# The first FFN product of the front tokens: seven-product units replaced by plain blocks

## The chip, the cores and the metric

One core of a Trainium2 chip runs the whole program. The metric is device time in microseconds (us), the median of the runs shown. The engines are TensorE (PE; its weight loads are listed as PEld), VectorE (DVE), ScalarE (ACT), GpSimd (POOL) and SyncE (SP, which here only issues DMAs).

## The reference

x has 2048 tokens of width 640; all inputs are bf16. There are 32 heads of width 20, and the FFN is 1728 wide.

```
xn = layernorm(x)                                  # no weights
q, k, v = split(xn @ wqkv)                         # 32 heads
phi(t) = where(t > 0, t + 1, exp(t)) + 1e-6
kv = phi(k)^T v ;  z = sum over tokens of phi(k)   # per head
o = (phi(q) kv) / (phi(q) z + 1e-6)
s = o @ wo
g = silu(relu(xn @ w1) @ w2)
out = x + s * g
```

## The kernel before, in words

Tokens are cut into 16 tiles of 128 (t) and 4 chunks of 512 (j). The 1728 FFN features are 13 full blocks of 128 (f = 0 to 12, `NF` = 13) and 64 odd ones. The width 640 is 5 blocks of 128 (k), so a plain product of one feature block with one chunk is 5 matmuls of 128x128 by 128x512 into one of 8 PSUM banks.

A small scheduler (`Sched`) takes operations in the order in which the Python code gives them, queues each on its engine, and derives the waits from named resources (`R` is what an operation reads, `W` what it writes; `hz` gives the last readers and writers of a buffer that is used again). Each engine and each DMA queue works strictly in this written order; nothing is planned beyond it. PE is in order too.

Work that matters here:

- `LN_stats(t)`: two statistics (L469) and their combination (L473) on VectorE, then two small POOL steps (L475, L477) that make `rsy`, the reciprocal standard deviation. `LN_norm(t)` (L497) writes the normed tile `xn` on VectorE, and a DMA transpose on SP (`xnT_dma`, L546) turns it into `xnT`, features by tokens.
- Tiles 0 to 3 (chunk 0) take a quicker way at the start: they are centred only, transposed on TensorE and copied to `xcT`. What is made from `xcT` lacks the factor `rsy`, so it is scaled later. `scale_rows` and `scale_bcast` spread `rsy` of these 512 tokens over all partitions (`rsyB`), and `scale_h(f)` multiplies a feature block of the hidden layer by it on VectorE.
- A key tile: `K_mm(t)` (L556, 10 matmuls of 320 columns into two banks), `K_exp` and `K_relu` on ScalarE (L569), `K_fin` on VectorE (L585, L587).
- A query block: `Q_mm` (L609, 5 matmuls), exp and relu on ScalarE (L617, L622), two sums on VectorE.
- A plain FFN block: `H_mm` or `H_block` (L658, 5 matmuls), and relu from PSUM into `hT` on ScalarE (L662). `H_half` (L676) makes the 64 odd features of two chunks in 20 narrow matmuls.
- A seven-product unit: `h_unit(i, jp)` makes the feature blocks i and i + 6 for the two chunks 2jp and 2jp + 1 by a two-by-two scheme of Strassen's kind (Winograd's form). In place of the 20 matmuls of four plain blocks it has 18 (L1036; seven products of two, and the fifth k-block by itself in four matmuls), sums of weights (`h_S`) and of activations (`h_T`) on VectorE ahead, and copies and sums through PSUM behind (ScalarE L1042 and L1048; VectorE L827).

Before the change the order is: chunk 0 as far as the keys of tiles 0 to 3, from `xcT`; five plain FFN blocks of chunk 0 (f = 4, 5, 10, 11, 12, the list `HP`) from `xcT`; key tiles 4 to 7; the same five blocks of chunk 1; `H_half(0)`; two query blocks; four units `h_unit(0..3, 0)` for the front pair of chunks, with key tiles 8 to 11 and query blocks between their steps; key tiles 12 to 15 with query blocks; two query blocks of chunk 2. Then the second pair of chunks follows with six units `h_unit(0..5)`, and all the rest (the key-value products, the second FFN product and the output product, most of it on L882 in seven products too). A key tile that stands inside a unit carries one more matmul (L562, `whole`), which fills the rest of its bank.

The x loads go to 8 slots (`xin`); `xs(t)` tells which. The units need a buffer for their fifth product, `s5h`.

Of the kernel before, what the change touches and what calls it, by code (L numbers as in the profile page):

```python
# [208 lines left out]
def bass_recurrent_scan__linear_attn_block__dense_activation_relu__prompt_kernel(  # L209
# [107 lines left out]
    rsyH = nc.alloc_sbuf_tensor("rsyH", [P, 4], f16)  # L317
    rsyB = wv_flat[:, 2 * D:2 * D + 4 * P].bitcast(f16)
    s5h = [wv_flat[:, 0:1024].bitcast(f32), wv_flat[:, 2 * D + 4 * P:2 * D + 4 * P + 1024].bitcast(f32)]
# [49 lines left out]
    def xs(t):  # L369
        return t if t < XR else (t - 4) % XR  # L370

    def x_load(t, n=1, E="SP", extra=()):
        sl = xs(t)
        dma(E, lambda eng: eng.dma_start(xin[:, sl:sl + n, :],
                                         x2[P * t:P * (t + n), :].rearrange("(t p) n -> p t n", p=P)),
            W=[("xin", sl + i) for i in range(n)], extra=extra)
# [36 lines left out]
    w1_load(2, 3, "SP")  # L413
    w1_load(5, 6, "SP")
    x_load(4)
    x_load(5)
    w1_load(6, NW, "SP")
    x_load(6)
    x_load(7)
    for d in (0, 3):  # L420
        w1_load(d, d + 1, "SP")
# [29 lines left out]
    def build_mv6():  # L451
        for lo, n, off in ((0, 6, 0), (6, 2, P - 2 * DH)):
            mt = mv6[:, lo:lo + n]
            key = ("mv6", lo)
            sc.op("POOL", lambda eng, mt=mt: eng.memset(mt, SC), W=[key])
            sc.op("POOL", lambda eng, mt=mt, n=n, off=off: eng.affine_select(
                out=mt, in_=mt, compare_op=ALU.is_ge, fill=0.0, base=-off, pattern=[[-DH, n]], channel_multiplier=1),
                R=[key], W=[key])
            sc.op("POOL", lambda eng, mt=mt, n=n, off=off: eng.affine_select(
                out=mt, in_=mt, compare_op=ALU.is_ge, fill=0.0, base=off + DH - 1, pattern=[[DH, n]], channel_multiplier=-1),  # L460
                R=[key], W=[key])

    build_consts()

    def bn(t, a):
        xv = xin[:, xs(t), :]
        sc.op("DVE", lambda eng: eng.bn_stats(stats[:, t, a, :], xv[:, HN * a:HN * (a + 1)]),  # L469
              R=[("xin", xs(t))], W=[("stats", t, a)])  # L470
# [16 lines left out]
    def LN_norm(t):  # L487
        if t >= 99:
# [4 lines left out]
                out=xn[:, t, :], in_=xin[:, xs(t), :], func=ACTF.Identity, bias=rsv[:, t:t + 1],  # L493
                scale=rsy[:, t:t + 1]), R=[("xin", xs(t)), ("rsv", t), ("rsy", t)], W=[("xn", t)])
# [3 lines left out]
            out=xn[:, t, :], in0=xin[:, xs(t), :], scalar1=mv[:, t, 0:1], scalar2=rsy[:, t:t + 1],  # L498
            op0=ALU.subtract, op1=ALU.mult), R=[("xin", xs(t)), ("mv", t), ("rsy", t)], W=[("xn", t)])
        xnT_dma(t)  # L500
# [6 lines left out]
    def mean_act(t, lo):  # L507
        junk = ek[:, eks(t), 0, 0:D - lo]
        sc.op("ACT", lambda eng: eng.activation(out=junk, in_=xin[:, xs(t), lo:D], func=ACTF.Copy, scale=1.0 / D,
                                                accum_out=msum[:, t, 1:2]),  # L510
              R=[("xin", xs(t))], W=[("msum", t, 1), ("ek_e", eks(t))])
# [39 lines left out]
    def K_mm(t, b, k0=0, k1=C, halves=(0, 1), whole=False):  # L551
# [9 lines left out]
        if whole:  # L561
            fns.append(lambda eng: eng.matmul(ps[b][:, HN:512], lhsT=one, rhs=wk[:, 0, 0:512 - HN], start=False, stop=True,  # L562
                                              skip_group_check=True))
# [101 lines left out]
    def H_half(jp, b=None):  # L665
# [3 lines left out]
        for u in range(2):  # L669
            keys += [("xnT", 4 * (2 * jp + u) + q) for q in range(4)]  # L670
        for k in range(C):
            for u in range(2):
                src = xnT[:, 2 * jp + u, :, :]
# [6 lines left out]
        for u in range(2):  # L680
            rows = slice(64 * u, 64 * (u + 1))
            sc.op("ACT", lambda eng, rows=rows, u=u: eng.activation(
                out=(hTh if jp + u == 0 else hT)[rows, NF, schunk(2 * jp + u)], in_=ps[b][rows, :], func=ACTF.Relu),
# [255 lines left out]
    def scale_rows():  # L939
        sc.op("POOL", lambda eng: eng.tensor_copy(rsyH[:, :], rsy[:, 0:4]), R=[("rsy", t) for t in range(4)], W=[("rsyH",)])  # L940

    def scale_bcast(b):
        sc.group("PE", [(lambda eng, t=t: eng.matmul(
            ps[b][:, P * t:P * (t + 1)], lhsT=rsyH[:, t:t + 1].to_broadcast([P, P]), rhs=ident[:, :],
            start=True, stop=True)) for t in range(4)], R=[("rsyH",), ("ident",)], W=[("ps", b)])
# [41 lines left out]
    def h_T(i, jp=1):  # L987
        j0, j1 = 2 * jp, 2 * jp + 1
        xall = [("xnT", t) for t in range(8 * jp, 8 * jp + 8)]
        B11, B21, B12, B22 = xnT[:, j0, 0:2, :], xnT[:, j0, 2:4, :], xnT[:, j1, 0:2, :], xnT[:, j1, 2:4, :]  # L990
# [11 lines left out]
    def h_unit(i, jp=1):  # L1002

        j0, j1 = 2 * jp, 2 * jp + 1
        xall = [("xnT", t) for t in range(8 * jp, 8 * jp + 8)]
# [17 lines left out]
            1: (z([blk(0, 0), blk(0, 1)], xb(j0, 0)), w),  # L1023
            2: (z([blk(0, 2), blk(0, 3)], xb(j0, 2)) + last(0, j0), w),
            3: (z(ws(4), xb(j1, 2)) + last(0, j1), w + [sk(4)]),
            4: (z([blk(1, 2), blk(1, 3)], tv(4)) + last(1, j0), w + [("hTs", 4)]),
# [3 lines left out]
            8: (last(1, j1), w),  # L1030
# [14 lines left out]
        def relu(E, f, j, b):  # L1045
            dst = (hT if j else hTh)[:, f, schunk(j)]
# [11 lines left out]
        def s5_():  # L1058
            mm(5, bc, True)
            cp(s5, skey, bc, ())  # L1060
# [5 lines left out]
        def s2():  # L1066
            mm(2, bb)
            relu("ACT", i, j0, bb)
# [5 lines left out]
        def s3():  # L1074
            mm(3, bc)
            relu("ACT", i, j1, bc)

        def s4():
            mm(8, ba)
            dst = hT[:, i + 6, schunk(j1)]  # L1080
            tt(dst, ps[ba], s5, ALU.add, [("ps", ba), skey], [("hT", j1, i + 6)])
            sc.op("DVE", lambda eng: eng.tensor_scalar(out=dst, in0=dst, scalar1=0.0, scalar2=None, op0=ALU.max),
                  R=[("hT", j1, i + 6)], W=[("hT", j1, i + 6)])
            mm(4, bd)
            relu(("ACT", "DVE")[jp], i + 6, j0, bd)
# [3 lines left out]
    HP = (4, 5, 10, 11, 12)  # L1089

    def K_tile(t, b):
        K_mm(t, b)
        K_exp(t, b)
        K_relu(t, b)

    def run(ops):
        for op_ in ops:
            op_[0](*op_[1:])

    S, N, F, SH, ZS, T0 = LN_stats, LN_norm, K_fin, h_S, scale_h, h_T  # L1100
    after = [[(S, 5), (N, 4)], [(S, 6), (N, 5)], [(S, 7), (N, 6)], [(F, 0), (N, 7)], [(F, 1)]]
    for n, f in enumerate(HP):
        H_block(0, f)
        run(after[n])
        if n == 3:
            x_load(8, 2)
            w_load(wq[:, :, :], A_wqkv[:, 0:D], ("wq",))
    scale_rows()
    after = [[(F, 2), (N, 0), (N, 1)], [(F, 3), (N, 2), (N, 3), (F, 4)], [(F, 5), (SH, 0, 1), (S, 8)],
             [(SH, 0, 3), (SH, 0, 2), (F, 6)]]  # L1110
    for n in range(4):
        K_tile(4 + n, 2 * (n % 2))
        run(after[n])
    x_load(10, 2)
    after = [[(N, 8), (F, 7), (SH, 0, 4)], [(S, 9), (T0, 1, 0), (T0, 3, 0)], [(N, 9), (T0, 2, 0)],
             [(T0, 4, 0), (S, 10)], [(ZS, 4), (ZS, 5)]]
    for n, f in enumerate(HP):
        if n == 2:
            scale_bcast(3)
        H_mm(1, f, (4, 5, 6, 7, 2)[n])()  # L1120
        if n == 1:
            x_load(12, 2)
            x_load(14, 2)
            for d in (1, 4):
                w1_load(d, d + 1, "SP")
        run(after[n])
    H_half(0, 3)
    pend = []

    def Q_late(j, f, b):  # L1130
        e, f_ = Q_mm(j, f, b)
        e()
        pend.append(f_)

    def Q_fins():
        while pend:
            pend.pop(0)()

    Q_late(0, 0, 0)
    Q_late(0, 1, 1)  # L1140
    units = [h_unit(i, 0) for i in range(4)]
    qfill = [(0, 2), (0, 3), (0, 4), (1, 0)]
    first = [[(N, 10)], [(N, 11)], [(N, 12)], [(N, 13), (N, 14)]]
    misc = [[(S, 11)], [(SH, 1, 1), (SH, 1, 3), (SH, 1, 2), (SH, 1, 4)], [(S, 13)], [(S, 15)]]
    post = [[], [(S, 12)], [(S, 14)], [(N, 15)]]
    units[0]["s1"]()
    for i, u in enumerate(units):
        ob = 4 * (i % 2)
        t = 8 + i
        u["s5"]()  # L1150
        K_mm(t, ob + 2, whole=True)
        K_exp(t, ob + 2)
        u["s6"]()
        K_relu(t, ob + 2)
        Q_fins()
        run(first[i])
        K_fin(t)
        u["s2"]()
        e2, f2 = Q_mm(*qfill[i], ob)
        u["s7"]()  # L1160
        run(misc[i])
        u["s3"]()
        if i < 3:
            units[i + 1]["s1"]()
        else:
            K_mm(12, 6)
        e2()
        u["s4"]()
        f2()
        run(post[i])  # L1170
    build_mv6()
    rest = [[(ZS, 10), (ZS, 11), (ZS, 12)], [(T0, 1), (T0, 3)], [(T0, 2)], [(T0, 4)]]
    for i in range(4):
        b = (6, 2, 0, 2)[i]
        if i:
            K_mm(12 + i, b)
        K_exp(12 + i, b)
        K_relu(12 + i, b)
        Q_block(1, 1 + i, 4 + i)
        K_fin(12 + i)  # L1180
        run(rest[i])
    Q_late(2, 0, 1)
    Q_late(2, 1, 3)
# [53 lines left out]
    for i, u in enumerate(units):  # L1237
# [9 lines left out]
        Q_fins()  # L1247
# [312 lines left out]
    for fn in stA[3:]:  # L1560
        fn()
        if fn.__name__ == "s2":
            g_T4()
            for i in range(1, 5):
                g_S(1, i)
    stB = seven(0, gprod(1), gout(1), 1, sx)
    for n, fn in enumerate(stB):
        fn()
        if n == 2:
            w_load(wv_sb[:, :, :], A_wqkv[:, 2 * D:3 * D], ("wv",), extra=hz([("rsyB",), ("s5h", 0), ("s5h", 1)]), E="ACT")  # L1570
# [126 lines left out]
```

## Time and profile before

| | before |
|---|---|
| median of 3 runs | 208.49 us (207.95 to 208.57) |
| the profiled execution | 208.57 us |
| its span, first to last instruction | 207.0 us |
| granted TensorE clock | 1.00 |
| TensorE busy | 203.6 us, 98% of the span |
| weight loads busy | 126.3 us, 61% |
| VectorE busy | 169.7 us, 82% |
| ScalarE busy | 124.3 us, 60% |
| POOL busy | 18.0 us, 9% |
| DMA | 24.74 MB, mean 119 GB/s |

A profile is of one execution. Busy times are shares of the span and overlap between engines. The chain of work that ended last is followed back from the last instruction: it names, for each moment, the work that the end of the program depended on. A group of instructions lists line, engine, operation, output and inputs, shape and count, then busy time, mean length of one, and the idle time of the engine ahead of them. Matmuls are pipelined and their ends are modelled, so the records of two that follow each other overlap.

### The profile page before, as it was taken

How to read it: one execution, taken by the hardware profiler on the slowest of the kernel's cores; microseconds unless marked ns; L12 is line 12 of the kernel's file. 1: busy time of each engine (PE TensorE's matmuls, PEld its weight loads, DVE VectorE, ACT ScalarE, POOL GpSimd, SP SyncE). 2: the span in 40 equal slices, each digit the busy share in tenths (PEclk: the TensorE clock that was granted, in tenths of full speed). 3: DMA queues.
4: the chain of work that ended last, by engine and by line, in shares of the span. 5: the costliest groups of instructions: out<-in, count | busy, mean ns of one | idle time of the engine just before them, and what ended most of it. 6: DMA issues, size and time to landing. Idle time of an engine off the chain costs nothing.

```text
span 207.0 us, 3745 instructions
## 1 busy us (share of the span) xinstructions
PE 203.6 (98%) x1400; PEld 126.3 (61%) x1400; DVE 169.7 (82%) x373; ACT 124.3 (60%) x251; POOL 18.0 (9%) x53
## 2 busy tenths in 40 slices
PE   8999999999999999999999999999999999999995
PEld 7755645545555444444456777777777777777773
DVE  4888997988969787686889669898888989897465
ACT  5598869888889987686563435462525354352531
POOL 3174032101330000000000000000000000000001
PEclk9999999999999999999999999999999999999999
DMA  6965999211037000302225999237931011010103
GB/s 194 331 190 117 255 203 275 42 32 29 6 63 198 25 3 0 127 0 57 74 63 114 251 357 384 90 108 234 371 129 63 3 63 46 21 63 0 63 5 127
DMA packets 32999, 24.74 MB, mean 119 GB/s; under 512 B 12757, under 2 KB 32981, under 8 KB 32981
## 3 DMA queue, kind: packets, MB, share of 16 engines
q1 hardware_dynamic: 31749, 23.13, 39.2%
q10 hardware_dynamic: 1232, 1.37, 1.9%
q8 instruction: 11, 0.18, 0.4%
q14 instruction: 7, 0.06, 0.1%
HBM read 15.81 MB, written 5.24 MB: 102 GB/s over the span
## 4 chain that ended last, share of the span: by engine, by line
PE 97%; DMA 1%; DVE 1%; issue 0%
PE psT L882 40%; PE psT L1036 19%; PE psT L556 11%; PE psT L609 11%; PE psT L658 6%; PE psT L1529 3%; PE psT L1580 2%; DMA reg<-in_A_x_dram 1%; PE psT L676 1%; PE psT L1320 1%; PE psT L530 1%; PE psT L1294 1%; PE psT L756 1%; PE psT L786 1%; PE psT L432 0%; DVE stats L469 0%
## 5 line engine op out<-in xcount | busy, mean ns | idle before, releaser
L882 PE MATMUL psT<-reg,regH 128*128 128x320 bf16 (+1 forms) x224 | 34.3, 299 | 0.0
L882 PE MATMUL psT<-reg 128*128 128x320 bf16 (+1 forms) x164 | 27.7, 299 | 0.0
L882 PEld LDWEIGHTS psT<-reg,regH 128*128 128x128 bf16 (+1 forms) x224 | 21.9, 98 | 8.6
L1354 ACT ACTIVATE wv_sb<-psT 128x320 bf16<-128x320 f32 x28 | 11.3, 436 | 25.2 <-PE psT L882 15.4
L609 PE MATMUL psT<-reg 128*128 128x512 bf16 x100 | 24.4, 379 | 0.0
L1036 PE MATMUL psT<-reg 128*128 128x512 bf16 x80 | 23.2, 379 | 0.0
L827 DVE TENSOR_TENSOR psT<-psT,reg 128x320 f32<-128x320 f32 x30 | 14.3, 493 | 9.3 <-PE psT L882 9.2
L889 ACT ACTIVATE psT<-psT 128x320 f32<-128x320 f32 x32 | 13.6, 426 | 11.2 <-PE psT L882 10.7
L882 PEld LDWEIGHTS psT<-reg 128*128 128x128 f16 (+1 forms) x164 | 16.0, 98 | 6.9 <-DVE regH L827 0.2
L889 ACT ACTIVATE reg<-psT 128x320 f32<-128x320 f32 (+1 forms) x24 | 10.4, 435 | 15.6 <-PE psT L882 13.6
L556 PE MATMUL psT<-reg 128*128 128x320 bf16 x120 | 17.9, 299 | 0.0
L1042 ACT ACTIVATE psT<-psT 128x512 f32<-128x512 f32 x20 | 11.9, 595 | 8.2 <-PE psT L1036 8.2
L569 ACT ACTIVATE regE<-psT 128x640 bf16<-128x640 f32 x24 | 15.6, 706 | 1.9 <-PE psT L556 1.2
L609 PEld LDWEIGHTS psT<-reg 128*128 128x128 bf16 x100 | 9.6, 98 | 11.6 <-issue 0.7
L1048 ACT ACTIVATE regH<-psT 128x512 bf16<-128x512 f32 (+1 forms) x24 | 14.5, 604 | 2.1 <-PE psT L1036 1.8
L556 PEld LDWEIGHTS psT<-reg 128*128 128x128 bf16 x120 | 11.5, 98 | 6.5 <-ACT regE L569 0.5
L469 DVE BATCH_NORM_STATS2 stats<-reg 128x6 f32<-128x320 bf16 x32 | 14.1, 475 | 1.3 <-DMA reg<-in_A_x_dram 1.3
L827 DVE TENSOR_TENSOR reg<-reg 128x1024 f16<-128x1024 bf16 (+6 forms) x17 | 13.5, 805 | 1.7 <-DMA reg<-in_B_w_dram 1.2
L882 PE MATMUL psT<-reg,pqT 128*128 128x320 bf16 (+1 forms) x72 | 14.7, 299 | 0.0
L1517 DVE TENSOR_TENSOR reg<-psT,wv_sb 128x640 bf16<-128x640 f32 (+2 forms) x16 | 11.8, 739 | 3.0 <-PE psT L882 1.8
L1036 PEld LDWEIGHTS psT<-reg 128*128 128x128 bf16 x80 | 7.7, 98 | 9.4 <-issue 0.4
L1522 POOL TENSOR_TENSOR reg<-reg 128x224 bf16<-128x224 bf16 x1 | 0.6, 607 | 144.0 <-DVE reg L1517 144.0
(143 smaller groups left out, 369.0 us busy)
## 6 DMA issues: line engine op xcount, KB each, us to landing
reg<-in_B_w_dram SPq DMA_DIRECT2D x12, 320.0 KB, 5.5
scr<-rden SPq DMA_DIRECT2D x4, 640.0 KB, 8.3
reg<-in_A_x_dram SPq DMA_DIRECT2D x4, 640.0 KB, 6.6
out_dram<-reg SPq DMA_DIRECT2D x15, 160.0 KB, 1.9
regE<-scr SPq DMA_DIRECT2D x3, 640.0 KB, 7.5
reg<-in_A_x_dram SPq DMA_DIRECT2D x4, 320.0 KB, 4.4
reg<-in_A_wo_dram SPq DMA_DIRECT2D x6, 160.0 KB, 3.3
reg<-in_A_x_dram SPq DMA_DIRECT2D x5, 160.0 KB, 5.5
```

The lines of the kernel that those rows point to most:

```text
L469: sc.op("DVE", lambda eng: eng.bn_stats(stats[:, t, a, :], xv[:, HN * a:HN * (a + 1)]), R=[("xin", xs(t))], W=[("stats", t, a)])
L556: fns.append(lambda eng, a=a, k=k, lhs=lhs: eng.matmul(ps[b + a][:, 0:HN], lhsT=lhs, rhs=wk[:, k, HN * a:HN * (a + 1)], start=(k == 0), st ...
L569: sc.op("ACT", lambda eng: eng.activation(out=o_.rearrange("p (a n) -> p a n", a=2), in_=ps2(b, HN), func=func, scale=scale), R=[("ps", b) ...
L609: sc.group("PE", [(lambda eng, k=k: eng.matmul(ps[b], lhsT=wq[:, k, P * f:P * (f + 1)], rhs=xnT[:, j, k, :], start=(k == 0), stop=(k == C ...
L658: sc.group("PE", [(lambda eng, k=k: eng.matmul(ps[b], lhsT=w1_col(k, P * f, P), rhs=src[:, k, :], start=(k == 0), stop=(k == C - 1))) for ...
L827: sc.op("DVE", lambda eng: eng.tensor_tensor(out=out, in0=in0, in1=in1, op=op), R=R, W=W, extra=extra)
L882: sc.group("PE", [(lambda eng, k=k, lhs=lhs, rhs=rhs: eng.matmul(ps[b][:, 0:HN], lhsT=lhs, rhs=rhs, start=(start and k == 0), stop=(k == n ...
L889: sc.op("ACT", lambda eng: eng.activation(out=dst, in_=ps[b][:, 0:HN], func=ACTF.Copy), R=[("ps", b)], W=[dkey], extra=extra)
L1036: sc.group("PE", [(lambda eng, k=k, lhs=lhs, rhs=rhs: eng.matmul(ps[b], lhsT=lhs, rhs=rhs, start=(start and k == 0), stop=(k == n - 1), sk ...
L1042: sc.op("ACT", lambda eng: eng.activation(out=dst, in_=ps[b], func=ACTF.Copy), R=[("ps", b)], W=[dkey], extra=extra)
L1048: sc.op("ACT", lambda eng: eng.activation(out=dst, in_=ps[b], func=ACTF.Relu), R=[("ps", b)], W=[("hT", j, f)])
L1517: sc.op("DVE", lambda eng: eng.tensor_tensor(out=tmpo[:, os_, lo:hi].rearrange(shp, a=na), in0=src, in1=g_of(t)[0][:, lo:hi].rearrange(shp ...
```

## The change

The change is named "last sum of w2 put behind the masking of the key-value products; zero rows of the FFN block filled by VectorE in its idle head in place of GpSimd", in place of "first FFN product of all chunks mostly in seven products". In the source it does this:

- The units of the front pair of chunks (`h_unit(i, 0)`, `h_T(i, 0)`) are gone. All 13 blocks of chunks 0 and 1 are plain blocks; chunk 0 takes all of them, and its half of the odd features, from `xcT`.
- The front is written as two loops. The first runs over the 13 blocks of chunk 0, with norms, statistics and key tiles 4 to 7 (behind blocks 5, 7, 9, 11) between. The second runs over 23 items, the 13 blocks of chunk 1 and ten query blocks, with key tiles 8 to 15 (behind items 2, 5, 8, 11, 14, 16, 18, 20), `H_half(0)` behind item 6, the scaling of chunk 0's blocks, and the `h_S` and `h_T` sums for the second pair.
- Key tiles in the front use banks 0 and 1 alone, and have no extra matmul.
- `scale_rows` is one POOL multiply of 128x512 (identity times `rsy`), and `scale_bcast` one matmul of 512 columns in place of four of 128. `scale_h` runs for all 13 blocks, and for the odd features later, in the first key-value unit.
- The masks (`build_consts`, which now holds `build_mv6` too) are built on POOL at the start of the second loop, in place of POOL's head and of the time behind the front units.
- All w1 loads are issued at the start, in order of the features; the x loads of tiles 8 to 15 are single, each behind the norm that frees its slot; the transposes of tiles 0 to 3 stand behind blocks 8 to 11 of the first loop.
- One of the two `s5h` buffers moves to the x slots 6 and 7.

The diff, cut to its core:

```diff
-    rsyH = nc.alloc_sbuf_tensor("rsyH", [P, 4], f16)
     rsyB = wv_flat[:, 2 * D:2 * D + 4 * P].bitcast(f16)
-    s5h = [wv_flat[:, 0:1024].bitcast(f32), ...]
+    dg = wv_flat[:, 2 * D + 4 * P:2 * D + 8 * P].bitcast(f16)
+    s5h = [reg7[:, 6 * D:6 * D + 1024].bitcast(f32), ...]
...
-    w1_load(2, 3, "SP")
-    w1_load(5, 6, "SP")
+    w1_load(0, 2, "SP")
     x_load(4)
     x_load(5)
-    w1_load(6, NW, "SP")
+    w1_load(2, 3, "SP")
     x_load(6)
     x_load(7)
-    for d in (0, 3):
-        w1_load(d, d + 1, "SP")
+    w1_load(3, NW, "SP")
...
-    build_consts()
...
-        xnT_dma(t)
+        if t >= 4:
+            xnT_dma(t)
+        if t + XR < T:
+            x_load(t + XR)
...
     def scale_rows():
-        sc.op("POOL", lambda eng: eng.tensor_copy(rsyH[:, :], rsy[:, 0:4]), ...)
+        sc.op("POOL", lambda eng: eng.tensor_tensor(
+            out=dg.rearrange("p (t n) -> p t n", t=4), in0=ident[:, :].unsqueeze(1).to_broadcast([P, 4, P]),
+            in1=rsy[:, 0:4].unsqueeze(2).to_broadcast([P, 4, P]), op=ALU.mult), ...)
...
-    HP = (4, 5, 10, 11, 12)
...
-    for n, f in enumerate(HP):
-        H_block(0, f)
-        run(after[n])
...
-    for i, u in enumerate(units):
-        ob = 4 * (i % 2)
-        t = 8 + i
-        u["s5"]()
-        K_mm(t, ob + 2, whole=True)
...
+    plans = [[("h", 0, f) for f in range(NF)], [], [], []]
...
+    for f in range(NF):
+        plans[1].append(("h", 1, f))
+        if ql and f > 1:
+            plans[1].append(("q",) + ql.pop(0))
+    kat = [{5: 4, 7: 5, 9: 6, 11: 7}, {2: 8, 5: 9, 8: 10, 11: 11, 14: 12, 16: 13, 18: 14, 20: 15}]
+    lnat = [{9: 8, 11: 9}, {0: 10, 2: 11, 5: 12, 8: 13, 11: 14, 13: 15}]
+    sums = {9: [(h_S, 0, 1), (h_S, 0, 2)], 10: [(h_S, 0, 4)], 12: [(h_S, 1, 1), (h_S, 1, 2)], 13: [(h_S, 1, 4)],
+            15: [(h_S, 0, 3)], 18: [(h_T, 1), (h_T, 3)], 19: [(h_T, 2), (h_T, 4), (h_S, 1, 3)]}
+    for j in range(2):
+        for n, item in enumerate(plans[j]):
+            if item[0] == "q":
+                Q_block(item[1], item[2])
+            else:
+                H_block(item[1], item[2])
+            if n in lnat[j]:
+                LN_stats(lnat[j][n])
+            if j == 1 and n == 0:
+                scale_bcast()
+                build_consts()
+            if j == 1 and n >= 7 and n < 20:
+                scale_h(n - 7)
...
+            if n in kat[j]:
+                t = kat[j][n]
+                K_mm(t, 0)
+                K_exp(t, 0)
+                K_relu(t, 0)
+                K_fin(t)
+            if j == 1 and n == 6:
+                H_half(0)
...
         if fn.__name__ == "s2":
             g_T4()
+            scale_h(NF)
...
-            w_load(wv_sb[:, :, :], ..., extra=hz([("rsyB",), ("s5h", 0), ("s5h", 1)]), E="ACT")
+            w_load(wv_sb[:, :, :], ..., extra=hz([("dg",), ("rsyB",), ("s5h", 1)]), E="ACT")
```

## The prediction

> **What bounds the kernel now.** I read the page's head, then the chain of work that ended last, first as shares and then in order of time, then the busy times by stage, and last the groups of instructions by shape.
>
> ```profile
> PE 203.6 (98%) x1400; PEld 126.3 (61%) x1400; DVE 169.7 (82%) x373; ACT 124.3 (60%) x251; POOL 18.0 (9%) x53
> ...
> PE 97%; DMA 1%; DVE 1%; issue 0%
> ```
>
> TensorE is on the chain for 97% of the span; the other engines do not end any stage. A busy share of TensorE could still hide waits inside matmuls, so the chain in order of time must say at what rate the matmuls go (columns: start, length, what; xN is the number of matmuls).
>
> ```profile
> 12.58 5.40 PE psT L658 x25
> 17.97 2.72 PE psT L556 x20
> 20.72 2.89 PE psT L556 x20
> 23.61 2.16 PE psT L658 x10
> 25.99 3.24 PE psT L658 x15
> 29.23 1.19 PE psT L676 x20
> ...
> 33.55 1.42 PE psT L556 x10
> 35.05 1.08 PE psT L1036 x5
> 36.13 1.08 PE psT L609 x5
> 37.21 2.81 PE psT L1036 x13
> ...
> 70.28 0.86 PE psT L1036 x4
> ```
>
> L658 is a plain FFN block, L1036 a product of a seven-product unit, L609 a query block, L556 a key tile. 5.40/25, 2.81/13 and 1.08/5 all give 0.216 us for a 512-wide matmul, whichever line issued it; 2.72/20 gives 0.136 us for a 320-wide one. 70.28 is the first matmul of the unchanged second half. From 12.58 on each piece starts where the last ended, so what TensorE is given is what the front lasts. The stages (columns: stretch, length, then busy time of PE, PEld, DVE, ACT, POOL, then clock, DMA share, GB/s):
>
> ```profile
> 12.58:23.61 11.03, 11.00 (x66) 6.18 (x65) 9.94 (x29) 9.70 (x16) 4.50 (x10) 1.00 0.58 136
> 23.61:30.42 6.81, 6.81 (x51) 2.97 (x49) 6.57 (x19) 4.66 (x8) 1.53 (x3) 1.00 1.02 235
> 30.42:32.69 2.27, 2.27 (x13) 1.02 (x12) 1.77 (x4) 2.17 (x4) 0.86 (x1) 1.00 1.03 240
> 32.69:70.28 37.59, 37.59 (x207) 19.98 (x206) 31.90 (x84) 32.70 (x61) 5.91 (x18) 1.00 0.35 81
> ```
>
> TensorE has 0.03 us idle in these 57.7 us, at full clock. VectorE is next: 50.2 us of 57.7.
>
> **The two edits in the change's name** are in both kernels alike: the last sum of w2 stands behind the masking in the loop over pairs, and the zero rows are a VectorE memset (L401). They cost nothing. The diff itself takes the seven-product form away from the first FFN product of token chunks 0 and 1.
>
> **TensorE, the sum.** Work between 12.58 and 70.28 before:
> - 512-wide matmuls: 50 of the ten plain blocks, 4 units of 18 = 72, 12 query blocks of 5 = 60; 182 x 0.216 = 39.31
> - 12 key tiles of 10: 120 x 0.136 = 16.32
> - the odd 64 features (L676): 1.19; the spread of the row scales (L943, 25.77 to 25.99): 0.22
> - 4 extra matmuls L562 in the key tiles of the units: 0.08 each (33.55 + 1.42 = 34.97, next piece at 35.05), 0.32
>
> That is 57.36; the front lasts 57.70, so 0.34 is small waits (a key tile at 2.89 where 2.72 is its rate, another at 1.42 where 1.36 is).
>
> After: a unit of 18 becomes 2 blocks x 2 chunks x 5 = 20 matmuls, so 130 block matmuls and 60 query matmuls: 190 x 0.216 = 41.04; the key tiles 16.32; the odd features 1.19; the spread of scales is now one 512-wide matmul, 0.216; no L562. Sum 58.77, that is +1.41 on 57.36. If the old small waits come back in like size the front grows by 1.41; if they vanish, because key tiles are now spread between blocks, by 58.77 - 57.70 = 1.07. I take +1.2.
>
> **VectorE** loses four sums of 128x1024 (`h_T` of the front pair, 0.69 each, 2.75), four PSUM adds (0.70), four adds into hT (0.68) and four maxima (0.29), 9.4 us in all. It gains 8 more scalings of chunk 0 in the front (0.41 each by the 128x512 f16 row of L827, 3.3 us): 44 us of 58.8. ScalarE loses two evictions a unit (0.6 each): 4.8 us. Neither was the bound; both reliefs are worth nothing while TensorE is full. The cover is real only if VectorE's order does not hold TensorE up, so I walked it: by the steps of its timeline a tile's statistics take 1.0, a norm 0.37, a key sum 0.76, a query sum 0.66, a scaling 0.36, an `h_S` sum 0.4. The heaviest stretch is items 8 to 13 of the second loop, where these add up to some 11.8 us beside 9.2 us of TensorE; the backlog of 2.6 us is mostly worked off by item 16, and no matmul before item 20 (key tile 15, normed at item 14) needs what stands in it.
>
> **Key tiles and transposes.** Key tile 4 is due at 12.58 + 6 x 1.08 = 19.06, instead of 17.97, tiles 5 to 7 each 3.52 later (two blocks and a tile), the loop ends at 32.06, and key tile 8 is due at 32.06 + 3.24 + 0.22 = 35.5. Transposes took 2.6 us at least, 2.7 in the median, 6.3 at most from issue to landing. Tile 4's was issued at 14.58. Two more weight loads (640 KB, 1.9 us at the 330 GB/s of 9.4 to 12.6) are ahead of it in the queue, which before ran empty by about 14, so now by about 16: landing near 18.5, 0.6 us in hand. Tile 8's is queued on SP behind x loads (0.58 us each) and the transposes of tiles 0 to 2 (1.26 each), and behind VectorE's norm of tile 8, itself behind the sums of key tile 6 (ScalarE done near 28.9): issued near 30.6, landed near 33.4, 2 us in hand. So nothing is added in my value; up to 1.8 us once (14.58 + 6.3 against 19.06) is kept for the range. Weight block d3 (features 6, 7) is due at 20.4, d0 when d2 was due before, in the same queue place. The x loads of tiles 12 to 15 wait on SP for the norms of tiles 4 to 7, as the transposes ahead of them do; what is behind them (wq, tiles 8 to 11) is due over 5 us later.
>
> **POOL.** The head masks (1.5 us, in POOL's idle head before) and the key-value masks (1.0 us, at 59 before) both move to the start of the second loop, 2.4 us in all, and the scales are spread by one POOL multiply of 128x512 (not in the trace; between the 0.18 of the cast that it replaces and, scaled by width from the 0.61 of 128x224, 1.4; I take 1.4, the same kind of instruction). Behind them on POOL stand `rsy` of tiles 8 and 11, due 2 to 5 us later. Cost 0; if the cover failed, 1 to 2 us.
>
> The row on sharing: POOL's `rsv` step took 0.22 us in quiet and up to 0.65, `rsy` 0.57 and up to 0.86, beside a busy VectorE. Read the other way round, VectorE could lose as much as all the moved POOL time, 2.4 + 1.4 = 3.8 us, of its 58.8 - 44 = 14 us idle: no cost either. The Trainium skill (SBUF — State Buffer, "Who interferes with whom") has the rule behind it, an exclusive lock on a shared port pair where the second to issue blocks fully; by it the sum is +1.2 too, unless the block falls on the norm of tile 8, which these rows can't show.
>
> **Later.** The scaling of the odd features (0.41) is now on VectorE between two long sums at about 114, where its next wait, at 119.4, was 1.96 us long: covered. The ACT-queued load of wv now waits for it too; it was issued at 118.3, well after. The half-unit buffer moved to xin slots 6 and 7 is free once tiles 14 and 15 are normed, long before. Nothing of the second half's TensorE work changes: it shifts.
>
> **Sum.** Profiled execution: 207.0 span, 208.57 in time, so 1.57 around the span; the median is 208.49. 207.0 + 1.2 + 1.57 = 209.8 against the profiled one, 209.7 against the median.
>
> **The rivals.**
> - **Late operands (0.15).** One or two transposes land late and TensorE stands: 1.2 + 1.8 = 3.0, 211.5; with tile 8 as well (30.6 + 6.3 = 36.9 against 35.5), 212.9. For it: 0.6 us in hand at tile 4. Against: the queue is quiet from 16 on.
> - **The plain blocks are cheaper (0.04, faster).** By the groups of instructions a unit's product costs more than a plain one:
>
> ```profile
> L609 PE MATMUL psT<-reg 128*128 128x512 bf16 x100 | 24.4, 379 | 0.0
> L1036 PE MATMUL psT<-reg 128*128 128x512 bf16 x80 | 23.2, 379 | 0.0
> ```
>
> 23.2/80 = 0.290 against 24.4/100 = 0.244. If that were the cost of a place on the array, 72 x 0.290 = 20.9 would become 80 x 0.244 = 19.5, and with the 0.32 of L562 the time falls by 1.7, to 206.8. It decides if units run above 0.23 us a matmul. Against: the pieces of the chain, 13 in 2.81 us; ends of matmuls are modelled in these rows, and a unit's groups of two and three end more often than groups of five.
> - **Matmuls are hidden (0.08).** The eight extra ones cost nothing, about 208.5. For it: weight loads fill only 61% of the span, and a matmul's own record is 379 ns, so the records overlap and their 98% need not mean full. Against: the gapless chain at 0.216 us a matmul. The Trainium skill (Perfetto Trace Analysis, "Identifying the Most-Contended Engine") speaks for this rival: it rates matmul busy time as no good measure and takes the weight-load share instead; by it alone the sum would be 0.
>
> **How the numbers follow.** The likeliest case, +1.07 to +1.41 (209.5 to 209.9), has 0.73. A measurement of this kernel can tell 0.3% from no change, 0.63 us. Faster by more: 0.05, the second rival and a little more. Within: 0.10, mostly the third. Slower by more: 0.85. The range goes from 208.9, which leaves out the second rival and most of the third, to 211.6, the first rival's one late transpose.
>
> **What would show it.** Right: no L1036 before the second half; 65 matmuls of L658's kind between 12.6 and about 32 with four key tiles between; the first L1036 at 71.3 to 71.7; TensorE without idle time; VectorE 6 us less busy ahead of it. Wrong: the same first product at 70.3 or less; a gap ahead of key tile 4 or 8 with a transpose as its releaser; TensorE waiting on VectorE in the second loop; a growth behind 71 instead of ahead of it.

## The result, and the profile after

The changed kernel took 209.85 us (median of four, 209.70 to 210.26) against 208.51 us before: the ratio is 1.0073, 95% interval 1.0051 to 1.0096. It is slower by 1.3 us; 209.7 was forecast. A second comparison (told below) gave 1.0039, 1.0020 to 1.0058. The profiled execution took 209.83 us, of which 208.3 are its span.

The page of the changed kernel:

```profile
PE 204.0 (98%) x1401; PEld 126.3 (61%) x1401; DVE 164.8 (79%) x366; ACT 120.8 (58%) x243; POOL 19.4 (9%) x53
...
PE 94%; DMA 2%; DVE 1%; issue 0%; SPq 0%
```

VectorE and ScalarE have 4.9 and 3.5 us less to do, and the kernel is slower all the same: TensorE is still what the end depends on. (Line numbers shift: L650 is a plain FFN block here, L1029 a product of a unit, L551 a key tile, L601 a query block, L939 the spread of the row scales.) The chain of waits of the changed kernel, in order of time (start, length, what):

```profile
12.67 6.47 PE psT L650 x30
19.14 1.36 PE psT L551 x10
20.50 2.16 PE psT L650 x10
22.66 1.36 PE psT L551 x10
...
31.05 2.16 PE psT L650 x10
33.21 0.22 PE psT L939
33.43 2.16 PE psT L650 x10
35.59 1.36 PE psT L551 x10
...
71.49 0.86 PE psT L1029 x4
```

All 26 front blocks are plain, at 6.47/30 = 0.216 us a matmul; no key tile starts late; the second half's first product comes at 71.49 instead of 70.28. Cut at the same two places, the stages of the changed kernel (stretch, length, then busy time of PE, PEld, DVE, ACT, POOL, clock, DMA share, GB/s):

```profile
12.67:71.49 58.82, 58.82 (x332) 30.73 (x331) 46.40 (x128) 45.50 (x80) 15.51 (x38) 1.00 0.49 114
71.49:112.98 41.49, 41.49 (x269) 19.76 (x267) 31.57 (x60) 29.22 (x56) 0.00 (x0) 1.00 0.15 44
112.98:208.30 95.32, 92.73 (x708) 67.23 (x705) 77.72 (x151) 38.08 (x92) 0.61 (x1) 1.00 0.42 134
```

and of the kernel before:

```profile
12.58:70.28 57.70, 57.67 (x331) 30.16 (x330) 50.18 (x133) 49.22 (x88) 12.79 (x32) 1.00 0.50 116
70.28:111.77 41.49, 41.49 (x268) 19.78 (x267) 32.97 (x64) 29.21 (x56) 0.00 (x0) 1.00 0.15 44
111.77:207.00 95.23, 92.73 (x707) 67.23 (x705) 77.53 (x150) 38.09 (x92) 0.61 (x1) 1.00 0.42 134
```

The front grew from 57.70 to 58.82, by 1.12 us. The middle stage has 41.49 us in both, to the hundredth, and TensorE's work in the rest is 92.73 in both. The spans are rounded to a tenth. By the last pieces of the chains, which end at 206.54 and 205.31 us, the whole grew by 1.23 us: 1.12 in the front, 0.09 at the head (the first FFN matmul comes at 12.67 instead of 12.58) and 0.02 behind 71.49.

### The profile page after: what moved, and what is told of

Read it like the earlier page. It is cut to its first block, busy times and chain, and to the rows that moved or that the text cites. A ratio compares the mean times of both kernels' runs of the same rounds, so it can differ in the third digit from the quotient of the medians.

```text
span 208.3 us, 3731 instructions
## 1 busy us (share of the span) xinstructions
PE 204.0 (98%) x1401; PEld 126.3 (61%) x1401; DVE 164.8 (79%) x366; ACT 120.8 (58%) x243; POOL 19.4 (9%) x53
## 4 chain that ended last, share of the span: by engine, by line
PE 94%; DMA 2%; DVE 1%; issue 0%; SPq 0%
PE psT L874 39%; PE psT L650 15%; PE psT L1029 11%; PE psT L601 10%; PE psT L551 10%; DMA reg<-in_A_wqkv_dram 2%; PE psT L1538 2%; PE psT L1486 2%; PE psT L668 1%; DVE reg L1474 1%; PE psT L1277 1%; PE psT L1251 1%; PE psT L748 1%; PE psT L778 1%; DVE reg L1479 0%
## 5 line engine op out<-in xcount | busy, mean ns | idle before, releaser
L819 DVE TENSOR_TENSOR psT<-psT,reg 128x320 f32<-128x320 f32 (+1 forms) x33 | 16.4, 513 | 11.7 <-PE psT L874 8.8
L601 PE MATMUL psT<-reg 128*128 128x512 bf16 x100 | 24.7, 380 | 0.0
L650 PE MATMUL psT<-reg 128*128 128x512 bf16 x75 | 18.5, 379 | 0.0
L654 ACT ACTIVATE regH<-psT 128x512 bf16<-128x512 f32 x28 | 16.5, 608 | 3.2 <-PE psT L650 3.2
L551 PE MATMUL psT<-reg 128*128 128x320 bf16 x120 | 18.3, 299 | 0.0
L601 PEld LDWEIGHTS psT<-reg 128*128 128x128 bf16 x100 | 9.6, 98 | 11.1 <-issue 0.7
L551 PEld LDWEIGHTS psT<-reg 128*128 128x128 bf16 x120 | 11.7, 98 | 6.5
L650 PE MATMUL psT<-regX,reg 128*128 128x512 bf16 x65 | 14.8, 379 | 0.0
L1029 PE MATMUL psT<-reg 128*128 128x512 bf16 x48 | 14.0, 379 | 0.0
```

Source lines behind the costliest of these rows:

```text
L551: fns.append(lambda eng, a=a, k=k, lhs=lhs: eng.matmul(ps[b + a][:, 0:HN], lhsT=lhs, rhs=wk[:, k, HN * a:HN * (a + 1)], start=(k == 0), st ...
L601: sc.group("PE", [(lambda eng, k=k: eng.matmul(ps[b], lhsT=wq[:, k, P * f:P * (f + 1)], rhs=xnT[:, j, k, :], start=(k == 0), stop=(k == C ...
L650: sc.group("PE", [(lambda eng, k=k: eng.matmul(ps[b], lhsT=w1_col(k, P * f, P), rhs=src[:, k, :], start=(k == 0), stop=(k == C - 1))) for ...
L654: return lambda: sc.op("ACT", lambda eng: eng.activation(out=hT[:, f, schunk(j)], in_=ps[b], func=ACTF.Relu), R=[("ps", b)], W=[("hT", j, f)])
L819: sc.op("DVE", lambda eng: eng.tensor_tensor(out=out, in0=in0, in1=in1, op=op), R=R, W=W, extra=extra)
L1029: sc.group("PE", [(lambda eng, k=k, lhs=lhs, rhs=rhs: eng.matmul(ps[b], lhsT=lhs, rhs=rhs, start=(start and k == 0), stop=(k == n - 1), sk ...
```

## The experiments

The theory is the prediction's: the front lasts as long as its matmuls, 0.216 us for each of 512 columns, and nothing else in the change reaches the end. The rivals are those of the prediction: matmuls that are hidden, plain blocks that are cheaper, operands that land late. The number that tells most is the length of the front, from the first FFN matmul to the second half's first product; it is read from the chain of each profile, or from TensorE's records where the chain does not pass there, and starts where the key matmuls ahead of it end.

| run | front, us | against its own parent | time: ratio to before, 95% interval |
|---|---|---|---|
| before | 57.70 | | |
| changed | 58.82 | +1.12 | 1.0073 (1.0051 to 1.0096) |
| changed, again | 58.82 | +1.12 | 1.0039 (1.0020 to 1.0058) |
| changed, eight matmuls fewer | 57.09 | -1.73 | 0.9965 (0.9944 to 0.9986) |
| before, eight more, first time | 61.23 | +3.53 | 1.0104 (1.0061 to 1.0148) |
| before, eight more, again | 59.37 | +1.67 | 1.0086 (1.0055 to 1.0117) |
| changed, masks early | 58.82 | 0.00 | 1.0059 (1.0035 to 1.0083) |
| changed, POOL multiply x4 | 58.82 | 0.00 | 1.0075 (1.0052 to 1.0098) |
| changed, wq early | 61.03 | +2.21 | 1.0156 (1.0124 to 1.0188) |
| before, key tiles in other banks | 58.26 | +0.56 | 1.0046 (1.0020 to 1.0073) |
| the same, and tiles 4 to 7 spread | 58.51 | +0.81 | 1.0035 (1.0005 to 1.0065) |
| before, two key tiles in other banks | 57.48 | -0.22 | 1.0012 (0.9987 to 1.0037) |

**Eight matmuls fewer in the changed kernel.** The fifth k-block of eight plain blocks is left out:

```diff
         src, keys = hsrc(j)
+        n_ = C - 1 if j == 1 and f < 8 else C
...
-                                                         start=(k == 0), stop=(k == C - 1))) for k in range(C)],
+                                                         start=(k == 0), stop=(k == n_ - 1))) for k in range(n_)],
```

> The changed kernel, with the fifth k-block of feature blocks 0 to 7 of chunk 1 left out: eight 512-wide matmuls fewer, all else the same (those blocks of h lack a fifth of their sum). Theory (the time is the count of matmuls at 0.216 us each): 8 x 0.216 = 1.73 us less than the changed kernel's 209.85, so 208.1, span near 206.6. Rival (matmuls are hidden, the loss comes from order, waits or transfers): 209.85, and TensorE gets idle time ahead of 71 us.

The times were 0.9963 (0.9945 to 0.9980) of before, median 207.87. The one profiled execution took 433.7 us, so its profile says nothing on the stages; the kernel was run once more for one, beside the changed kernel itself:

> The changed kernel with the fifth k-block of feature blocks 0 to 7 of chunk 1 left out, once more, for a profile. Theory: 1.73 us less than the changed kernel beside it, all of it ahead of the second half: its first product at 71.49 - 1.73 = 69.76, behind it the same lengths. Rival (hidden): 71.5.

> The changed kernel as it is, beside the two runs with eight matmuls fewer and more, on one chip. Theory: 1.3 us over the kernel before (ratio 1.006), second half's first product near 71.5.

Stages of the run with eight fewer (columns as above; a few matmul records are missing, which is why PE busy is below the length):

```profile
12.30:69.39 57.09, 56.67 (x318) 29.97 (x323) 46.52 (x128) 45.46 (x80) 16.05 (x39) 1.00 0.55 119
69.39:110.88 41.49, 41.10 (x264) 19.80 (x267) 31.55 (x60) 29.23 (x56) 0.00 (x0) 1.00 0.16 44
```

58.82 - 57.09 = 1.73 us = 8 x 0.216: each matmul left out is won in full in the front. The median fell to 207.93 beside 209.36 for the changed kernel, 1.4 us. Hidden matmuls are ruled out. The profiled execution itself took 208.55 us, only 0.85 less than that of the changed kernel beside it (209.40). The front won 1.73, but behind it this execution lost 0.86: TensorE stood for the load of wv, as its chain shows:

```profile
117.45 11.25 DMA wv_sb<-in_A_wqkv_dram
128.69 0.14 issue
128.83 1.59 PE psT L1252 x30
```

In the two profiles of the changed kernel itself this load took 9.1 and 9.6 us, and TensorE did not wait for it. What made it longer here was not followed.

The changed kernel in this second comparison stood only 0.85 us over before by the medians (209.36 against 208.51), with the same front, 58.82; its first FFN matmul came at 12.28 us instead of 12.67. That is 0.39 of the 0.43 us between its two profiled executions (209.83 and 209.40).

**Eight matmuls more in the kernel before.** Each front unit issues its first product twice into the same bank, the second time with a fresh start:

```diff
             l_, R = prod[q]
+            if q == 1 and jp == 0:
+                l_ = l_ + l_
             n = len(l_)
...
-                ps[b], lhsT=lhs, rhs=rhs, start=(start and k == 0), stop=(k == n - 1), skip_group_check=True))
+                ps[b], lhsT=lhs, rhs=rhs, start=(start and k in (0, n - 2)), stop=(k == n - 1), skip_group_check=True))
```

> The kernel before, each of the four front units with its first product issued twice into the same bank (the second start clears the first): eight 512-wide matmuls more, no other instruction. Theory: 208.51 + 1.73 = 210.2, span near 208.7, the second half's first product at 72.0 instead of 70.28. Rival (hidden): 208.5. Rival (a unit's matmul costs 0.290, a plain one 0.244): + 2.3, so 210.8.

In its first profile TensorE also stood twice for a transpose. TensorE in order of time, that run (the bracket is idle time, and what ended it):

```profile
29.94 1.26 PE L676 MATMUL psT<-reg 128*32 128x512 bf16 x20 [0.60 <-DMA reg<-reg]
...
35.79 0.43 PE L556 MATMUL psT<-reg 128*128 128x320 bf16 x2 [1.02 <-DMA reg<-reg]
```

61.23 - 57.70 = 3.53 us, of which 1.73 are the matmuls and most of the rest these two waits. The first wait ended at 29.94, ahead of any extra matmul (the first unit begins at 33.31), so these did not make it; whether they had a part in the second, whose transpose was issued at 29.09, this run alone does not say. So it was run again:

> The kernel before with its front units' first product issued twice, once more: in the first profile of it a transpose of tile 8 landed 6.6 us behind its issue and TensorE stood about 2.2 us ahead of key tile 8. Theory: without such a landing 1.73 us over the kernel before, first product of the second half at 72.0; with one up to 2.2 us more. If the late landing is in this profile too, it belongs to the kernel before and its order of loads, and not to chance.

```profile
12.18:71.55 59.37, 58.97 (x333) 31.09 (x338) 50.13 (x133) 49.54 (x88) 12.90 (x33) 1.00 0.50 115
71.55:113.04 41.49, 41.10 (x264) 19.78 (x267) 32.96 (x64) 29.23 (x56) 0.00 (x0) 1.00 0.15 44
```

Without the late landing the front is 1.67 us longer than before, against 1.73. A unit's step of 13 matmuls in 2.81 us became 15 in 3.24, 0.216 again:

```profile
37.19 3.24 PE psT L1038 x15
```

The rival that a unit's matmul costs 0.290 expected 2.3 and falls. By the time's interval, 1.0055 to 1.0117, alone (1.1 to 2.4 us) it would not have.

For tile 8 a landing as late as 6.6 us was seen once: in the other five profiles with this order of transposes (the kernel before, the second of these runs and the three with other banks below) it took 3.5 to 5.2 us. What made it late in the one is open. The margin in the kernel before was small. Its tile-8 transpose was issued at 28.10 and landed 5.2 us later, at 33.3, for a key tile that started at 33.55; 6.6 us, as in the first of these runs, is too late. In the changed kernel the same transpose was issued at 30.9 and landed in 2.6 us, at 33.5, for a key tile at 35.59.

**The late operands, made to happen.** In the changed kernel the load of wq goes ahead of the first transposes:

```diff
     w1_load(3, NW, "SP")
+    w_load(wq[:, :, :], A_wqkv[:, 0:D], ("wq",))
...
-                if n == 4:
-                    w_load(wq[:, :, :], A_wqkv[:, 0:D], ("wq",))
```

> The changed kernel, with the load of wq (800 KB) moved ahead of the first transposes, so that it stands in the queue before tile 4's: at the 330 GB/s of that stretch 2.4 us more. The transpose landed 3.2 us behind its issue at 14.68, that is at 17.9, 1.2 us ahead of key tile 4 (19.14). Theory (the rival of late operands, made to happen): landing at 20.3, TensorE stands 1.1 us ahead of key tile 4 and the time is 210.9. Rival (transposes are not held by loads queued ahead): 209.85.

TensorE in order of time:

```profile
12.04 6.64 PE L651 MATMUL psT<-regX,reg 128*128 128x512 bf16 x30
20.71 1.53 PE L552 MATMUL psT<-reg 128*128 128x320 bf16 x10 [2.03 <-DMA reg<-reg]
```

The transpose of tile 4 landed 6.4 us behind its issue instead of 3.2, and key tile 4 waited 2.0 us for it; the time went to 211.69. The mechanism of the rival is real, and its price (1.1 expected) was set too low: the DMA engines' share was still 1.28 between 18 and 20 us (the profile's count of it can pass 1), where the changed kernel had 0.79. In the changed kernel itself the same transpose had 1.2 us in hand (14.68 + 3.2 = 17.9, due 19.14).

**The masks back at POOL's head.** `build_consts()` stands ahead of the statistics again.

> The changed kernel, with the masks built on POOL at its idle head again, as before the change. Theory: POOL's steps at the start of the second loop are covered, time 209.85, span 208.3, the second half's first product at 71.5. Rival (the masks hold up rsy of a tile or block VectorE's port): faster, by up to 1 us, 208.9.

The front was 58.82 again, the first product of the second half at 71.50. The move of the masks costs nothing.

**The POOL multiply four times.**

```diff
-                scale_rows()
+                for _ in range(4):
+                    scale_rows()
```

> The changed kernel, with the POOL multiply that spreads the row scales (1.03 us in its profile) issued four times, into the same buffer: 3.1 us more on POOL behind 20.3 us. Theory: VectorE operations beside it are stretched or held, as the norm of tile 7 was in the changed kernel (1.16 us beside it, 0.4 otherwise); x loads 8 to 11 go out up to 3 us later, so the transpose of tile 8, which had some 2 us in hand, is 0 to 1 us late: 209.85 to 210.9. Rival (the two engines share nothing, the long norm was a wait of another kind): no VectorE operation is longer than in the changed kernel, 209.85.

VectorE in order of time, that run (start, length, line, operation):

```profile
18.01 0.32 DVE L577 TENSOR_SCALAR regE<-regE 128x640 bf16<-128x640 bf16 x1
18.37 0.49 DVE L579 TENSOR_TENSOR reg<-regE 128x640 bf16<-128x640 bf16 x1
19.32 1.15 DVE L489 TENSOR_SCALAR reg<-reg,mv,rsy 128x640 bf16<-128x640 bf16 x1 [0.46 <-POOL rsy L469]
20.40 1.19 DVE L577 TENSOR_SCALAR regE<-regE 128x640 bf16<-128x640 bf16 x1
21.63 1.25 DVE L579 TENSOR_TENSOR reg<-regE 128x640 bf16<-128x640 bf16 x1
22.80 1.16 DVE L577 TENSOR_SCALAR regE<-regE 128x640 bf16<-128x640 bf16 x1
23.99 0.49 DVE L579 TENSOR_TENSOR reg<-regE 128x640 bf16<-128x640 bf16 x1
```

and POOL in the same run:

```profile
19.26 4.52 POOL L934 TENSOR_TENSOR wv_sb<-ident,rsy 128x512 f16<-128x512 bf16 x4
```

Four VectorE operations beside four multiplies of 1.13 us took 1.15 to 1.25 us each, where they take 0.32 to 0.49 alone: each took 0.75 to 0.87 us longer, and about as long as one multiply. That fits the exclusive lock that the Trainium skill states (SBUF — State Buffer, "Who interferes with whom"), by which one engine holds the shared ports for its whole instruction and the other stands; it is seen here for a scalar and for a tensor form. These rows do not tell standing from running slower. TensorE did not notice: front 58.82, first product at 71.48, time 209.71.

**The extra matmuls of the kernel before.** The four extra matmuls (L562) are the only TensorE work that the change saved. Can the units do without them? The key tile inside a unit went to the two banks that are started afresh next:

```diff
-        K_mm(t, ob + 2, whole=True)
-        K_exp(t, ob + 2)
+        K_mm(t, ob + 1, halves=(1, 0), st=2)
+        K_exp(t, ob + 1, 2)
```

> The kernel before, without the four extra matmuls: the key tile inside a unit goes to the two banks whose next use starts afresh (ob+1 and ob+3, a stride of two), its halves in the other order. Theory: 4 x 0.08 = 0.32 us less, 208.2, span 206.7. Rival: bank ob+1 comes free later (VectorE reads it for the unit's last sum), TensorE waits for that by up to 0.3 us a unit, and nothing or less than nothing is won: 208.5 to 209.4.

It was slower, 1.0046. The chain of that run:

```profile
33.06 0.60 ACT pqT L619
33.66 0.05 issue
33.70 1.53 PE psT L556 x10
...
39.88 0.56 DVE regH L824
40.44 0.05 issue
40.49 1.53 PE psT L556 x10
```

Key tile 8 waits for ScalarE to clear a query block's bank, key tile 9 for VectorE's last sum of the unit before. The rival held: 58.26, 0.56 longer, although 0.32 of work was gone. (The wait for ScalarE it had not named.) With key tiles 4 to 7 spread over three pairs of banks besides, it was no better:

> As the run before it (key tiles of the units in banks ob+1 and ob+3), and key tiles 4 to 7 over three pairs of banks in place of two, with the banks of the five blocks behind them reordered. Theory: the waits of 0.03 and 0.17 us at key tiles 5 and 6 go too, 208.0, span 206.5. Rival: ScalarE's two evictions a tile (1.3 us) set the pace of these four tiles (1.36 us on TensorE each), and the wait only moves to the next tile or block: 208.2.

The median was 209.18 beside 209.12, the front 58.51: TensorE, 0.2 us earlier at the odd features because the waits at key tiles 4 to 7 were gone, stood 0.38 us there for a transpose. Since the waits stood at tiles 8 and 9, only tiles 10 and 11 were then moved:

> The kernel before, with only the key tiles of the third and fourth unit (tiles 10 and 11) in banks ob+1 and ob+3 and without the extra matmul; tiles 8 and 9 as before. In the run with all four moved the waits stood at tiles 8 and 9 alone, and tiles 10 and 11 came 6.33 us apart where the kernel before has 6.40. Theory: 0.16 us less, the second half's first product at 70.1, time 208.3, not to be told from 208.4. Rival: bank ob+1 comes free late at tile 10 too once tile 9 is early, and nothing is won.

The front is 57.48, 0.22 shorter, but the time is 208.52 beside 208.51 (1.0012, 0.9987 to 1.0037): nothing that a measurement of the time can tell. None of the three versions with other banks beats the kernel before by its time.

## Why the prediction was right, point by point

**TensorE, the sum.** The step carried. Work of 58.77 us was counted for the front; it lasted 58.82, and in four executions (the changed kernel twice, masks early, multiply x4) the same 58.82. The two runs with eight matmuls fewer and more gave 1.73 and 1.67 us for 8 x 0.216 = 1.73.

**The small waits.** +1.41 if the old waits of 0.34 us came back, +1.07 if not; 1.2 was taken. It was 1.12: most of them went, and 0.05 is left over the sum. Key tiles that stand between blocks, 3.52 us apart, give ScalarE time to clear the banks: the kernel before has two waits of a key tile for ScalarE's eviction (0.5 us of the weight loads), the changed kernel none. One of the small waits stayed, behind the odd features, where five query matmuls take 1.19 us in place of 1.08 (in the kernel before ten take 2.27 in place of 2.16); in the sum it is hidden by the rate, which is rounded up (6.47/30 is 0.2157).

**Head and tail.** They were not in the sum and made 0.11 us of the 1.23 by which the profiled chains differ. The front's first FFN matmul came between 12.04 and 12.68 us in these profiles, at 12.28 and 12.67 in two of the changed kernel itself, while the front was the same to the hundredth. By the chains it hangs on the first loads: that of the changed kernel runs through the load of wk until 6.61 us, that of the kernel before through a load of x. The tail can scatter too: the late load of wv cost 0.86 us in one profile. The front grew by 1.12 in both comparisons and gives 209.6 alone; the medians moved by 1.34 and by 0.85. So the front is the test of the sum; that one median came within 0.15 us of 209.7 is in part luck.

**VectorE and ScalarE.** The direction and the price, nothing, were right. VectorE's relief in the front was put at 6.1 us and is 50.18 - 46.40 = 3.8. Two parts were missed. The last key sum and one `h_T` sum, which the kernel before did mostly behind the second half's first product (from 70.17 us on), are now done ahead of it (32.97 - 31.57 = 1.4 us less behind). And the norm of tile 7 took 1.16 us instead of 0.4 beside POOL's multiply. ScalarE's 4.8 is right by the groups of instructions: the FFN evictions of the front fell from 34 with 20.1 us to 26 with 15.3. The stage's busy time counts records that overlap once, and fell by 3.7.

**Key tiles and transposes.** Tile 4: landing near 18.5 forecast, 17.9 measured. Tile 8: issue near 30.6 and landing near 33.4 forecast, 30.9 and 33.5 measured, 2.1 us in hand. Not seen ahead: VectorE stood 2.15 us for the load of tile 8, at 28.10. It is within that landing and cost nothing.

**POOL.** The multiply was put at 1.4 us between 0.18 and 1.4; it took 1.03.

**The rivals.** Late operands: not in the changed kernel, and shown as possible by the early load of wq. Plain blocks cheaper: refuted by the units with 15 matmuls in 3.24 us; the group's busy time divided by its count is no cost of a matmul. Hidden matmuls: refuted from both sides. The Trainium skill (Perfetto Trace Analysis, "Identifying the Most-Contended Engine") names two measures for TensorE, the matmul work done as a share of the peak and the share of weight loads. The prediction took the second alone for this rival; at 61% it did not show that the engine was full, and the chain without gaps did. The first was not worked out here.

## What to carry to other kernels

Where the chain of waits is one engine without gaps, count that engine's work and price it by the chain's own rate; relief elsewhere is worth nothing, and here 3.8 us of VectorE and 3.7 of ScalarE bought none. Work taken out of the full engine counts only if what replaces it makes it wait for nobody: four matmuls of 0.08 us were cheaper than moving all four key tiles to banks that made them needless (moving two won 0.22 us in the front, and nothing that the time shows). To see a change below half a percent, compare the length of the stage between two marks in the profile: here the head scattered by up to 0.64 us between profiles, and one late load behind the front cost 0.86.

## What the runs showed of the hardware that was not expected

- One execution of the kernel with eight matmuls fewer took 433.7 us. In its records matmuls took a little over double (30 plain ones in 14.11 us, 0.47 each; 402 of L875 in 117.42 us, where the changed kernel has 54.60) from the head to the end, with the granted clock shown as 1.00. VectorE and ScalarE kept their pace: a statistic took 474 ns and an FFN eviction 597 (475 and 608 in the changed kernel). The nineteen other executions of the same kernel took 207.4 to 208.6 us. The cause is open.
- A DMA transpose of one tile took from 2.6 to 6.6 us from issue to landing. Loads queued ahead are one cause: 3.2 for tile 4 in the changed kernel, 6.4 with 800 KB more ahead.
